# One list scheduler for a whole fused kernel: attention, experts and MLP ordered in three parts with shared state

## The chip, the cores and the metric

The kernel runs on one core of a Trainium2 chip. The metric is the device time of one execution in microseconds, median of several runs on the same chip. Before the change it is 509.02 us (three runs, 508.78 to 509.10). The engines are named as in the profile: PE (matrix products), PEld (loading of the stationary operand), DVE (vector), ACT (activations), POOL, and SP, whose queue starts the transfers.

## What is computed

Three layers follow each other, all in float32, for 4 batches of 448 tokens with 768 features (12 heads of 64):

```python
# attention, capped scores
scores = cap * tanh(q @ k.T * scale / cap)
attn = exp(scores - max) / (sum + 1e-9)
x = (attn @ v) with the heads side by side          # 4 x 448 x 768
# four experts, the best two of each token, causal attention of width 64 inside each expert
w = softmax over the two largest of x @ w_gate
ye = softmax(causal(scale * (x wq[e]) @ (x wk[e]).T)) @ (x wv[e]) @ wo[e]
out = sum over the two experts of w * ye
# gated MLP
h = gelu(out @ w_in); u, v = halves of h
v_n = layernorm(v) * g_ln;  v_s = w_sg @ v_n + b_sg
y = out + (u * v_s) @ w_out
```

## The kernel before

**Attention.** The 48 heads go as 24 pairs, one per `slot`. For a pair, `scores` writes four tiles `s` (three blocks of 128 keys, and one tile with the 64 tail keys of two pairs), ACT turns them into `p` with tanh (one per tile) and exp (one per two tiles), and `values` multiplies `p` with `v` into `po` one slot later. `pb` is the sum of `p` over key blocks (DVE, later POOL), and `sum` is its column sum on PE. Two buffers of PSUM hold `s`, one bank `po`, three the tiles named `g` (`sum`, `w2ps`, `qk`, `v`, `a`, `tr`, `av`, half of the `po`).

**Sub-arrays.** These products use a part of PE's 128 x 128 array and run beside each other: `s` on 64 rows by 128 columns (shown as 64\*128), tail scores and tail values on 64\*64, `po` on 128\*64, `sum` on 128\*32, `a` on 64\*112, `av` on 112\*64. The other products (`w2ps`, `qk`, `v`, and all of the MLP) take the whole array. A float32 product makes two records of the trace ("x4" is two products); `qk`, `v` and the MLP are sums of three products of rounded halves, one record each. A name like `s1_2_3` is batch 1, pair 2, tile 3; `tr0_0_1_2` is batch, expert pair, expert, chunk.

**Beside attention.** In the first 10 slots (`PRE_SLOTS`) `prepare_weights` converts the 64-bit `w_in` in twelve pieces (`wi0` to `wi11`, mostly on DVE) and PE multiplies each with `wo` into `w2ps`. In the slots after that `beside` runs the experts of the batch that is done (`queries_keys` `qk`, `values_chunk` `v`, `gates`, `weigh` `a`, `settle`, `turn` `tr`, `attend` `av`) after the table `PLAN`. `normed` inverts a batch's sums `rs` by way of DRAM (`rd`, `ri`, `rb`) and makes the experts' input `xh`, `xl`.

**What sets the order.** Each engine keeps the order in which the program issues its instructions (`InOrder`, which passes every instruction through one helper line, L338). Up to the last slot that is the order in which the Python code is written. Only the end (`experts_end` and `mlp`, from L1026 on) is recorded in the `Agenda` first: `order` holds estimated durations, buffers (`slots`), the shape that PE is in (`cfg`, 95 ns added where it differs, L226) and PE's bank, walks through estimated time and takes for each engine the instruction that can begin first; within 100 ns of each other PE takes one of the same bank, then the one with the longest chain behind it (`level`, L243). Transfers before the end are outside of it, and its start state is a guess (`since`, L345). All queues are in order: an instruction that waits holds back everything behind it on its engine.

Of the kernel before, what the change touches and what calls it, by code (L numbers as in the profile page):

```python
# [77 lines left out]
class Agenda:  # L78
# [24 lines left out]
    def add(self, eng, f, args, kw):  # L103
# [9 lines left out]
        for x, wr in [(x, False) for x in ins] + [(x, True) for x in outs]:  # L113
            t = x.tensor
            lo, hi, p0, p1 = self.span(x)
            for j, l, h, q0, q1, w in self.seen.setdefault(t.name, []):
                if (wr or w) and lo < h and l < hi and p0 < q1 and q0 < p1 and j != i:
                    after.add(j)
            if t.name not in self.uses:
                self.uses[t.name] = []  # L120
                if x.space != bass.MemoryType.DRAM and getattr(t, "tag", None) is not None:
                    self.caps.setdefault(t.cap_key, []).append((t.name, wr, t))
# [7 lines left out]
        op = dict(i=i, eng=eng, call=lambda: f(*args, **kw), after=after, tiles=set(tiles), took=[], port=False)  # L130
# [3 lines left out]
        if eng == "pe":  # L134
            st, mv = (args[1], args[1]) if name == "transpose" else (kw.get("lhsT", args[1]), kw.get("rhs", args[-1]))
            n = mv.free_size() if name != "transpose" else args[1].partition_size()
            op["dur"] = (96.0 if name == "transpose" else .446 * n + 3.5 if st.dtype == F32R else 2 * max(.825 * n, 185.0))
# [8 lines left out]
        elif eng == "dve":  # L146
# [5 lines left out]
            elif name in ("tensor_scalar", "tensor_copy") and not psum:  # L152
# [5 lines left out]
        else:  # L158
            op["dur"] = 450.0
            size = outs[0].partition_size() * outs[0].free_size() * 4 if outs[0].space != bass.MemoryType.DRAM else (  # L160
                ins[0].partition_size() * ins[0].free_size() * 4)
            op["bytes"] = size
            op["extra"] = 1500.0 if outs[0].tensor.name.startswith(("rb", "ri", "rd", "wo", "gln")) else 0.0
        self.ops.append(op)

    def order(self):
        ops, n = self.ops, len(self.ops)
        then = [[] for _ in ops]
        for op in ops:
            for j in op["after"]:  # L170
                then[j].append(op["i"])
        level = [0.0] * n
        for i in reversed(range(n)):
            op = ops[i]
            took = op["dur"] + self.LATENCY[op["eng"]]
            if op["eng"] == "sp":
# [3 lines left out]
            level[i] = took + max((level[j] for j in then[i]), default=0.0)  # L180
        slots, queue, where, left = {}, {}, {}, {t: len(set(u)) for t, u in self.uses.items()}
        for key, tiles in self.caps.items():
            cap = tiles[0][2].tag_meta.bufs
            old = [t for t, w, _ in tiles if not w]
            slots[key] = [0.0] * (cap - len(old)) + [None] * len(old)
            queue[key] = [t for t, w, _ in tiles if w]
            for t, w, _ in tiles:
                where[t] = (key, len(slots[key]) - 1 - old.index(t) if not w else None)
        need, ready, end = [len(op["after"]) for op in ops], [0.0] * n, [0.0] * n
        for op in ops:  # L190
            for t in op["tiles"]:
                for k, v in self.since.items():
                    if t.startswith(k) and where.get(t, (0, 0))[1] is not None:
                        ready[op["i"]] = max(ready[op["i"]], v)
        open_ = {}
        for t, u in self.uses.items():
            made = {i for i in u if ops[i]["eng"] == "pe" and ops[i]["bank"] == t}
            open_[t] = {j for i in made for j in ops[i]["after"] if ops[j]["eng"] != "pe"} or ({-1} if not made else set())
        feeds = [[] for _ in ops]
        for t, js in open_.items():  # L200
            for j in js - {-1}:
                feeds[j].append(t)
        free = dict.fromkeys(self.LATENCY, 0.0)
        pools = {e: [] for e in free}
        for op in ops:
            if not need[op["i"]]:
                pools[op["eng"]].append(op["i"])
        grid, cfg, bank, lock, pipe, done = [[0.0] * 4 for _ in range(4)], None, None, 0.0, 0.0, []

        def begin(i):  # L210
            op = ops[i]
            t = max(free[op["eng"]], ready[i])
            for x in op["tiles"]:
                key, s = where.get(x, (None, 0))
                if s is not None:
                    continue
                if queue[key][0] != x and (not x.startswith(self.fill) or open_[x] or sum(s is not None for s in slots[key]) < 2):
                    return None
                got = [s for s in slots[key] if s is not None]
# [1062 lines left out]
```

## Time and profile before

| | |
|---|---|
| runs | 508.78, 509.02, 509.10 us |
| profiled execution | 510.37 us, of which the span of the trace is 508.6 us |
| PE | 496.8 us busy (98%) |
| DVE, ACT | 330.8 and 329.0 us (65% each) |
| POOL | 94.2 us (19%) |
| chain that ended last | PE 72%, DVE 12%, ACT 7%, DMA 4% |
| granted PE clock | 1.0 in all slices |

The span is what the trace covers; 1.77 us of the execution lie outside of it. Products on PE overlap and their ends are modelled, so "busy" also hides short stops: the distance from one start to the next tells more than the durations do. Where PE was found idle, the profile names what ended the wait.

### The profile page before, as it was taken

To read this page: it belongs to the slowest core of one execution; us is meant where nothing else is said; L and a number is where in the kernel's file an instruction comes from. 1 tells how busy PE (TensorE), PEld (TensorE's weight loads), DVE (VectorE), ACT (ScalarE), POOL (GpSimd) and SP (SyncE) were. 2 spreads that over 40 slices of the span, in tenths; PEclk is the share of its full clock that TensorE was granted. 3 is DMA by queue.
4 is the path that set the end of the run, shared out by engine and by line. 5 is a ranking of instruction groups with operands and counts; after the bars stand their busy time and mean duration, and the time that the engine had idled before them with its cause. 6 is when DMAs were issued, how large, how long until landed. Compare 5 with 4: busy or idle time off the path is not lost.

```text
span 508.6 us, 7515 instructions
## 1 busy us (share of the span) xinstructions
PE 496.8 (98%) x2702; PEld 329.6 (65%) x2702; DVE 330.8 (65%) x719; ACT 329.0 (65%) x558; POOL 94.2 (19%) x103
## 2 busy tenths in 40 slices
PE   7999999999999999999999989999999999999997
PEld 2233333455555556655559777877799899989996
DVE  4899998992666664655664999847860594497050
ACT  6989989868788686678765757757831263355131
POOL 0000000133145152235063302031410010010000
PEclk9999999999999999999999999999999999999999
DMA  8974626885334142414023622015011001100212
GB/s 292 310 267 141 216 88 141 241 295 176 102 102 151 58 129 63 127 58 113 1 68 88 193 60 64 1 46 233 1 37 54 19 1 56 54 0 1 90 43 85
DMA packets 35188, 54.27 MB, mean 107 GB/s; under 512 B 5584, under 2 KB 30160, under 8 KB 35152
## 3 DMA queue, kind: packets, MB, share of 16 engines
q1 hardware_dynamic: 35008, 53.57, 33.4%
q8 instruction: 21, 0.34, 0.3%
q10 hardware_dynamic: 144, 0.23, 0.2%
q14 instruction: 15, 0.12, 0.1%
HBM read 42.04 MB, written 11.75 MB: 106 GB/s over the span
## 4 chain that ended last, share of the span: by engine, by line
PE 72%; DVE 12%; ACT 7%; DMA 4%; SPq 2%; issue 2%; POOL 0%; DVEq 0%; ACTq 0%; POOLq 0%
PE o L338 17%; PE s L338 8%; PE qk L338 8%; PE po L338 8%; PE sp L338 7%; PE v L338 6%; ACT p L338 4%; PE hu L338 3%; DVE pb L338 3%; PE a L338 3%; PE av L338 3%; PE tr L338 2%; DMA rb<-rd 2%; PE hv L338 2%; ACT pe L338 2%
## 5 line engine op out<-in xcount | busy, mean ns | idle before, releaser
L338 ACT ACTIVATE p<-s,tsc 128x896 f32<-128x896 f32 x84 | 80.9, 1006 | 20.3 <-PE s L338 20.0
L338 PE MATMUL s<-qp,kp 64*128 64x448 f32 (+1 forms) x384 | 79.1, 573 | 3.0 <-ACT p L338 3.0
L338 ACT ACTIVATE p<-p,capt 128x1792 f32<-128x1792 f32 (+1 forms) x48 | 77.0, 1603 | 1.1
L338 DVE TENSOR_TENSOR pb<-pb,p 128x896 f32<-128x896 f32 (+1 forms) x48 | 53.2, 1109 | 20.0 <-ACT p L338 10.7
L338 POOL TENSOR_TENSOR pb<-p 128x896 f32<-128x896 f32 x14 | 29.9, 2134 | 166.5 <-PE po L338 94.7
L338 PE MATMUL po<-p,vv 128*64 128x448 f32 x288 | 59.4, 548 | 0.0
L338 PEld LDWEIGHTS s<-qp,kp 64*128 64x128 f32 (+1 forms) x384 | 27.7, 176 | 48.4 <-issue 23.5
L338 ACT ACTIVATE ob<-o 128x448 f32<-128x448 f32 x24 | 12.9, 544 | 53.1 <-PE o L338 49.0
L338 DVE SCALAR_TENSOR_TENSOR vs<-sp,gln,bsg 128x448 f32<-128x448 f32 x16 | 10.6, 680 | 54.9 <-PE sp L338 54.7
L338 PEld LDWEIGHTS po<-p,vv 128*64 128x64 f32 x288 | 18.5, 136 | 37.9 <-issue 34.1
L338 DVE CUSTOM_DVE_ANT_0 a<-a,neg 112x112 f32<-112x112 f32 (+3 forms) x64 | 27.7, 468 | 20.8 <-PE a L338 20.2
L338 ACT ACTIVATE pe<-a,m 112x112 f32<-112x112 f32 (+3 forms) x64 | 31.1, 493 | 11.5 <-DVE m L338 11.5
L338 PE MATMUL qk<-xh,wqk_h 128*128 128x448 f32 x96 | 37.6, 391 | 0.1
L338 PE MATMUL o<-gh,wu_l 128*128 128x448 f32 x96 | 35.0, 365 | 0.0
L338 PE MATMUL o<-gl,wu_h 128*128 128x448 f32 x96 | 35.0, 364 | 0.0
L338 PE MATMUL qk<-xh,wqk_l 128*128 128x448 f32 x96 | 35.0, 364 | 0.0
L338 PE MATMUL o<-gh,wu_h 128*128 128x448 f32 x96 | 34.9, 364 | 0.0
L338 POOL TENSOR_TENSOR rstd<-rstd,mhalf 128x1 f32<-128x1 f32 (+1 forms) x16 | 10.8, 678 | 121.1 <-DVE rstd L338 119.2
L338 POOL TENSOR_SCALAR pe<-pe,cs 112x224 f32<-112x224 f32 (+3 forms) x40 | 24.1, 621 | 45.7 <-DVE cs L338 44.6
L338 PE MATMUL v<-wvg_h,xh 128*112 128x260 f32 x96 | 28.2, 294 | 1.4 <-ACT pe L338 1.3
L338 PE MATMUL v<-wvg_h,xl 128*112 128x260 f32 x96 | 27.1, 283 | 0.0
L338 PE MATMUL v<-wvg_l,xh 128*112 128x260 f32 x96 | 27.1, 282 | 0.0
(237 smaller groups left out, 1083.8 us busy)
## 6 DMA issues: line engine op xcount, KB each, us to landing
rb<-rd SPq DMA_DIRECT2D x24, 224.0 KB, 5.4
out_dram<-ob SPq DMA_DIRECT2D x24, 224.0 KB, 1.9
kp<-in_kT_dram SPq DMA_DIRECT2D x23, 224.0 KB, 3.0
qp<-in_qT_dram SPq DMA_DIRECT2D x23, 224.0 KB, 3.3
vv<-in_v_dram SPq DMA_DIRECT2D x24, 192.0 KB, 3.3
wuw<-in_w_out_dram SPq DMA_DIRECT2D x5, 384.0 KB, 5.0
wud<-wuw SPq DMA_DIRECT2D x10, 192.0 KB, 1.9
ws<-in_wqk_dram SPq DMA_DIRECT2D x4, 384.0 KB, 7.9
```

Source lines behind the costliest of these rows:

```text
L338: return tc.keep_in_program_order(f(*args, **kw))
```

## The change

All instructions are now recorded in the `Agenda`, in three runs that share its state (estimated free times, buffers, the shape and bank of PE, the transfer pipe): the first 10 slots, the slots after them, and the end. In the first two the key that breaks ties is the program's order, in the third it is `level` as before. Transfers are recorded too (SP still takes them in program order within 20 ns). A product that follows another one on PE counts from that one's estimated start and no longer from its end (`past`). Neighbouring products on a part of the array that fit beside each other form a `gang`; its first member may begin only when the inputs of all members are there. A program-order rule for writers of one tile on PE is added, and `settle` splits its work over three engines only in the end, as before. The helper line is L387 after the change.

```diff
             lo, hi, p0, p1 = self.span(x)
             for j, l, h, q0, q1, w in self.seen.setdefault(t.name, []):
-                if (wr or w) and lo < h and l < hi and p0 < q1 and q0 < p1 and j != i:
+                if j != i and (wr or w) and (lo < h and l < hi and p0 < q1 and q0 < p1 or
+                                             wr and w and name == "matmul" and self.ops[j]["eng"] == eng):
                     after.add(j)
...
+    def order(self, new, by_level, floor):
...
                 took = op["dur"] + (0.0 if any(ops[j]["eng"] == "pe" for j in then[i]) else 220.0)
-            level[i] = took + max((level[j] for j in then[i]), default=0.0)
-        slots, queue, where, left = {}, {}, {}, {t: len(set(u)) for t, u in self.uses.items()}
+            op["level"] = took + max((ops[j]["level"] for j in then[i]), default=0.0)
+            op["key"] = op["level"] if by_level else -op["rank"]
...
+        gang, team = {}, []
+        for i in new:
+            op = ops[i]
+            if op["eng"] != "pe":
+                continue
+            r, c, r0, c0 = op["cell"]
+            if (r, c) == (4, 4) or not team or (r, c) != ops[team[0]]["cell"][:2] or any(
+                    abs(r0 - ops[j]["cell"][2]) < r and abs(c0 - ops[j]["cell"][3]) < c for j in team):
+                team = []
+            team.append(i)
+            gang[i] = team
 
         def begin(i):
             op = ops[i]
-            t = max(free[op["eng"]], ready[i])
-            for x in op["tiles"]:
+            t, mates, new_tiles = free[op["eng"]], [i], {}
+            if i in gang and gang[i][0] == i:
+                mates = gang[i]
+                if any("end" not in ops[q] for j in mates for q in ops[j]["after"] if q not in mates):
+                    return None
+                t = max([t] + [self.past(q, j) for j in mates for q in ops[j]["after"] if q not in mates])
+            t = max(t, ready[i])
+            for x in (x for j in mates for x in ops[j]["tiles"]):
...
+            for j in mates if op["eng"] == "pe" else ():
+                r, c, r0, c0 = ops[j]["cell"]
+                if (r, c) != self.cfg and self.cfg:
+                    t = max(t, max(map(max, grid)) + 95.0)
                 else:
                     t = max(t, max(grid[y][x] for y in range(r0, r0 + r) for x in range(c0, c0 + c)))
             if op["port"]:
...
                 if e == "pe":
-                    t, i = max(near, key=lambda x: (ops[x[1]]["bank"] == bank, level[x[1]], -x[1]))
+                    t, i = max(near, key=lambda x: (ops[x[1]]["bank"] == self.bank, ops[x[1]]["key"], -x[1]))
                 elif e == "sp":
                     t, i = min(near, key=lambda x: x[1])
                 else:
-                    t, i = max(near, key=lambda x: (level[x[1]], -x[1]))
-                if best is None or t < best[0]:
+                    t, i = max(near, key=lambda x: (ops[x[1]]["key"], -x[1]))
+                if best is None or t < best[0] + (1.0 if e == "pool" else 0.0):
                     best = (t, i)
...
+    def past(self, j, i):
+        x, a, b = self.ops[j], self.ops[j]["eng"], self.ops[i]["eng"]
+        if a == b == "pe":
+            return x["at"]
+        return x["end"] + (0.0 if a == b and "bytes" not in x else self.LATENCY[a])
+
+    def run(self, by_level, floor=lambda key: 0.0):
...
             for i in range(NC):
                 pe = PES[b, ep, el, i]
-                by = "apavaaap"[4 * el + i] if agenda.on else "p"
+                by = "apavaaap"[4 * el + i] if agenda.end else "p"
                 if by == "a":
                     act.activation(pe, pe, AF.Copy, scale=cs[:, i:i + 1])
                 elif by == "v":
@@ -1011,8 +1060,12 @@
             for _ in range(int(WARM)):
                 mm(g, z[:, :128], z, start=True, stop=True)
         load_w, beside_pre = prepare_weights(pre)
+        agenda.on = True
+        agenda.free["pe"] = 3400.0
         for n in range(PRE_SLOTS):
             slot(n, beside_pre(n))
+        agenda.run(False, )
+        used = max(op["end"] for op in agenda.ops)
     ypool = ES(tc.tile_pool(name="ypool", bufs=3, reuse_waits="tile"))
     mo = ES(tc.tile_pool(name="mo", bufs=1, reuse_waits="tile"))
     sm = ES(tc.tile_pool(name="sm", bufs=2, reuse_waits="tile"))
@@ -1020,10 +1073,14 @@
     w2_t = [w2.tile([128, 2, FF], F32R, name=f"w2_{t}") for t in "hl"]
     w2_h, w2_l = w2_t
     YA = {}
+    agenda.on = True
     for n in range(PRE_SLOTS, B * HP + 1):
         slot(n, beside(n))
+    agenda.run(False, lambda key: used if str(key).split("_")[-2] in ("mo", "ypool", "w2") else 0.0)
+    closed = max(op["end"] for op in agenda.ops if any(t.startswith(("p", "kp", "s")) for t in op["tiles"]))
     ah.close()
-    agenda.on = True
+    agenda.on = agenda.end = True
+    agenda.fill = tuple(f"{t}{b}" for t in "ov" for b in range(B))
 
 
 
@@ -1222,7 +1279,7 @@
     agenda.hold(("wo", "wu_"), ("wqk", "wvg"))
     drain(mlp(((mlp_a, 0), (token_weights, 0), (mlp_weights, 2), (mlp_b, 0), (mlp_weights, 1), (mlp_a, 1), (mlp_b, 1),
                (mlp_a, 2), (mlp_b, 2), (mlp_a, 3), (mlp_b, 3), (mlp_c, 0), (mlp_c, 1), (mlp_c, 2), (mlp_c, 3))))
-    agenda.run()
+    agenda.run(True, lambda key: closed if str(key).split("_")[-2] in ("ml", "w4", "mr", "ps") else 0.0)
 
 
 def _rows(w):

```

Three places on PE show what the planner does. The first is the start of the program, from the tail scores of the first two pairs (`s0_0_3`) on; before:

```order
L338 MATMUL s0_0_3_172<-qp0_1_125,kp0_1_126 64x448 x2
L338 MATMUL s0_1_0_186<-qp0_1_125,kp0_1_126 128x448 x2
L338 MATMUL s0_1_1_190<-qp0_1_125,kp0_1_126 128x448 x2
L338 MATMUL po0_0_208<-p0_0_0_135,vv0_0_121 64x448 x4
L338 MATMUL po0_0_208<-p0_0_1_167,vv0_0_121 64x448 x2
L338 MATMUL s0_1_2_220<-qp0_1_125,kp0_1_126 128x448 x2
L338 MATMUL s0_2_0_232<-qp2_131,kp2_132 128x448 x2
L338 MATMUL s0_2_1_236<-qp2_131,kp2_132 128x448 x2
L338 MATMUL po0_0_208<-p0_0_1_167,vt0_0_123 64x448 x2
```

After:

```order
L387 MATMUL s0_0_3_130<-qp0_1_114,kp0_1_115 64x448 x2
L387 MATMUL po0_0_140<-p0_0_0_119,vv0_0_112 64x448 x4
L387 MATMUL s0_1_0_134<-qp0_1_114,kp0_1_115 128x448 x2
L387 MATMUL s0_1_1_135<-qp0_1_114,kp0_1_115 128x448 x2
L387 MATMUL po0_0_140<-p0_0_1_128,vv0_0_112 64x448 x2
L387 MATMUL po0_0_140<-p0_0_1_128,vt0_0_113 64x448 x2
L387 MATMUL po0_1_155<-p0_0_1_128,vt0_0_113 64x448 x2
L387 MATMUL s0_1_2_144<-qp0_1_114,kp0_1_115 128x448 x2
L387 MATMUL s0_2_0_148<-qp2_117,kp2_118 128x448 x2
```

The first values (`po0_0`, `po0_1` with the tail operand `vt`) moved ahead of the scores of pair 1 and of `s0_1_2`, in two pieces.

The second is about slot 8, where the products `w2ps` of the last pieces of `w_in` stand. Before, from the last score tile of pair 2 of batch 1:

```order
L338 MATMUL s1_2_3_691<-qp8_497,kp8_498 64x448 x2
L338 MATMUL s1_2_3_691<-qp9_564,kp9_565 64x448 x2
L338 MATMUL w2ps1_0_552<-wi9m_577,wt_108 128x512
L338 MATMUL w2ps1_1_553<-wi9m_577,wt_108 128x512
L338 MATMUL sum1_0_700<-pb1_0_520,onehot_71 32x448 x2
L338 MATMUL sum1_0_700<-pb1_1_590,onehot_71 32x448 x2
L338 MATMUL s1_3_0_715<-qp9_564,kp9_565 128x448 x2
L338 MATMUL s1_3_1_719<-qp9_564,kp9_565 128x448 x2
L338 MATMUL po1_2_734<-p1_2_0_640,vv1_2_605 64x448 x4
L338 MATMUL po1_2_734<-p1_2_1_686,vv1_2_605 64x448 x2
L338 MATMUL s1_3_2_752<-qp9_564,kp9_565 128x448 x2
L338 MATMUL w2ps1_0_552<-wi10m_609,wt_108 128x512
```

After, from the tile ahead of it:

```order
L387 MATMUL s1_2_3_271<-qp8_219,kp8_220 64x448 x2
L387 MATMUL s1_2_3_271<-qp9_237,kp9_238 64x448 x2
L387 MATMUL w2ps1_0_234<-wi10m_251,wt_108 128x512
L387 MATMUL w2ps1_0_234<-wi11m_260,wt_108 128x512
L387 MATMUL w2ps1_1_235<-wi11m_260,wt_108 128x512
L387 MATMUL po1_0_248<-p1_0_1_231,vt1_0_210 64x448 x2
L387 MATMUL po1_1_266<-p1_0_1_231,vt1_0_210 64x448 x2
L387 MATMUL po1_1_266<-p1_1_0_239,vv1_1_230 64x448 x4
L387 MATMUL po1_1_266<-p1_1_1_253,vv1_1_230 64x448 x2
L387 MATMUL sum1_0_272<-pb1_0_226,onehot_71 32x448 x2
L387 MATMUL sum1_0_272<-pb1_1_246,onehot_71 32x448 x2
L387 MATMUL s1_3_0_277<-qp9_237,kp9_238 128x448 x2
```

The products of `wi10` and `wi11` moved from behind `s1_3_2` to directly behind `s1_2_3`, and the values `po1_0`, `po1_1` from ahead of `s1_2_2` to behind them. On DVE the conversion of `wi11` now stands among the adds for `pb1_1`, with the subtraction `wqk_l` ahead of its end.

The third is in the experts of batch 0, second expert pair, where `qk0_1_0` and the transposes of the first pair `tr0_0_0` meet. Before:

```order
L338 MATMUL tr0_0_0_2_1282<-ident_73,pe0_0_0_2_1087 112x112 x3
L338 MATMUL qk0_1_0_1268<-xh0_745,wqk_h_76 128x448
L338 MATMUL qk0_1_0_1268<-xh0_745,wqk_l_77 128x448
L338 MATMUL qk0_1_0_1268<-xh0_745,wqk_h_76 128x448
L338 MATMUL qk0_1_0_1268<-xh0_745,wqk_l_77 128x448
L338 MATMUL tr0_0_0_3_1291<-ident_73,pe0_0_0_3_1121 112x112 x4
L338 MATMUL qk0_1_0_1268<-xh0_745,wqk_h_76 128x448
L338 MATMUL qk0_1_0_1268<-xh0_745,wqk_l_77 128x448
L338 MATMUL qk0_1_0_1268<-xl0_746,wqk_h_76 128x448 x6
L338 MATMUL sum2_0_1306<-pb2_0_972,onehot_71 32x448 x2
L338 MATMUL sum2_0_1306<-pb2_1_1097,onehot_71 32x448 x2
L338 MATMUL s2_3_0_1332<-qp15_1068,kp15_1069 128x448 x2
```

After:

```order
L387 MATMUL qk0_1_0_906<-xh0_285,wqk_l_77 128x448
L387 MATMUL qk0_1_0_906<-xl0_286,wqk_h_76 128x448 x6
L387 MATMUL tr0_0_0_0_908<-ident_73,pe0_0_0_0_835 112x112
L387 MATMUL tr0_0_0_0_908<-ident_73,pe0_0_0_1_846 112x112 x2
L387 MATMUL tr0_0_0_2_909<-ident_73,pe0_0_0_2_864 112x112 x3
L387 MATMUL s2_3_0_916<-qp15_856,kp15_857 128x448 x2
L387 MATMUL tr0_0_0_3_910<-ident_73,pe0_0_0_3_876 112x112 x4
L387 MATMUL sum2_0_911<-pb2_0_838,onehot_71 32x448 x2
L387 MATMUL sum2_0_911<-pb2_1_869,onehot_71 32x448 x2
L387 MATMUL s2_3_1_917<-qp15_856,kp15_857 128x448 x2
```

The transposes, which stood in three places among the products of `qk0_1_0`, now stand behind all 18 of them, and a score tile (`s2_3_0`) stands between two transposes and ahead of `sum2_0`.

## Rows read from the trace of the kernel before

**Rows 1.** The page, busy time of each engine over the whole span.
```profile
PE 496.8 (98%) x2702; PEld 329.6 (65%) x2702; DVE 330.8 (65%) x719; ACT 329.0 (65%) x558; POOL 94.2 (19%) x103
```

**Rows 2.** Busy time by stretch: its width, then each engine's busy us and instructions.
```profile
60.00:80.00 20.00, 20.00 (x97) 6.72 (x94) 19.25 (x31) 17.72 (x21) 0.00 (x0) 1.00 0.29 86
180.00:200.00 20.00, 19.55 (x130) 12.61 (x132) 9.39 (x26) 14.77 (x26) 10.44 (x13) 1.00 0.35 105
200.00:220.00 20.00, 19.67 (x129) 10.45 (x126) 10.36 (x34) 14.66 (x24) 7.59 (x10) 1.00 0.37 104
```

**Rows 3.** Timeline of PE at startup: start, duration (us), run of instructions, idle before it.
```profile
8.43 1.28 PE L338 MATMUL s<-qp,kp 64*64 64x448 f32 x8 [0.32 <-ACT p L338]
...
11.15 1.92 PE L338 MATMUL s<-qp,kp 64*128 64x448 f32 x8 [1.44 <-ACT p L338]
...
18.38 1.02 PE L338 MATMUL s<-qp,kp 64*128 64x448 f32 x4 [1.20 <-ACT p L338]
```

**Rows 4.** Timeline of PE, runs of products, each ahead of one of another shape.
```profile
49.81 1.02 PE L338 MATMUL s<-qp,kp 64*128 64x448 f32 x4
50.77 1.98 PE L338 MATMUL w2ps<-wi4m,wt 128*128 128x512 f32 x4
...
54.40 1.77 PE L338 MATMUL s<-qp,kp 64*128 64x448 f32 x8
56.10 0.98 PE L338 MATMUL po<-p,vt 64*64 64x448 f32 x8
57.01 2.48 PE L338 MATMUL po<-p,vv 128*64 128x448 f32 x12
59.42 1.94 PE L338 MATMUL s<-qp,kp 64*128 64x448 f32 x12
```

**Rows 5.** Timeline of PE and its weight loads, the first sums behind the experts' start.
```profile
102.28 1.98 PE L338 MATMUL sum<-pb,onehot 128*32 128x448 f32 x8
...
103.30 0.14 PEld L338 LDWEIGHTS sum<-pb,onehot 128*32 128x32 f32 x4 [0.89 <-DVE pb L338]
...
104.18 1.77 PE L338 MATMUL s<-qp,kp 64*128 64x448 f32 x8
```

**Rows 6.** Timeline of PE, transposes between products of `qk`.
```profile
144.18 0.45 PE L338 MATMUL tr<-ident,pe 112*112 112x112 f32 x3
144.41 0.45 PE L338 MATMUL qk<-xh,wqk_h 128*128 128x448 f32 x1
144.69 0.36 PE L338 MATMUL qk<-xh,wqk_l 128*128 128x448 f32 x1
144.89 0.36 PE L338 MATMUL qk<-xh,wqk_h 128*128 128x448 f32 x1
```

**Rows 7.** Timeline of PE in the last part, three of its waits.
```profile
295.36 0.36 PE L338 MATMUL hu<-yh,w_l 128*128 128x448 f32 x1
296.11 0.98 PE L338 MATMUL a<-qk 64*112 64x224 f32 x8 [0.39 <-ACT pt L338]
...
298.60 0.45 PE L338 MATMUL tr<-ident,pe 112*112 112x112 f32 x3
300.39 0.37 PE L338 MATMUL v<-wvg_h,xh 128*112 128x260 f32 x1 [1.33 <-ACT pe L338]
...
359.48 0.97 PE L338 MATMUL tr<-ident,pe 112*112 112x112 f32 x8
360.99 0.38 PE L338 MATMUL tr<-ident,pe 112*112 112x112 f32 x2 [0.54 <-ACT pt L338]
```

**Rows 8.** Timeline of PE and DVE, products of `w_in` and its last conversion.
```profile
79.67 1.98 PE L338 MATMUL w2ps<-wi9m,wt 128*128 128x512 f32 x4
...
80.95 0.69 DVE L338 TENSOR_TENSOR wi11m<-wi11m,wi11e 128x512 f32<-128x512 f32 x1
...
82.56 0.95 DVE L338 TENSOR_TENSOR wqk_l<-ws,wqk_h 128x768 fp32r<-128x768 f32 x1
...
89.36 1.88 PE L338 MATMUL w2ps<-wi11m,wt 128*128 128x512 f32 x4
```

More of the change, by code (lines that the diff above doesn't have):

```diff
@@ L82, with __init__ @@
     OVERLAP = {"act": 100.0, "dve": 80.0, "pool": 27.0, "sp": 0.0}
-    def __init__(self, tc, since):
-        self.tc, self.since = tc, since
-        self.ops, self.on = [], False
+    def __init__(self, tc):
+        self.tc = tc
+        self.ops, self.on, self.late, self.end = [], False, 0, False
         self.seen, self.uses, self.caps = {}, {}, {}
-        self.behind, self.fill = {}, tuple(f"{t}{b}" for t in "ov" for b in range(B))
+        self.behind, self.fill = {}, ()
+        self.slots, self.queue, self.where, self.left = {}, {}, {}, {}
+        self.free = dict.fromkeys(self.LATENCY, 0.0)
+        self.grid = [[0.0] * 4 for _ in range(4)]
+        self.cfg = self.bank = None
+        self.lock = self.pipe = 0.0
+        self.last, self.kept = {}, set()
     def hold(self, these, those):
@@ new lines, in order @@
+        slots, queue, where, left = self.slots, self.queue, self.where, self.left
+        keep = {t for tiles in self.caps.values() for t, _, _ in tiles[-tiles[0][2].tag_meta.bufs:]}
+        for t, u in uses.items():
+            left[t] = len({i for i in u if "end" not in ops[i]}) + (t in keep)
+            if t in self.kept and not left[t] and where.get(t, (0, None))[1] is not None:
+                key, s = where[t]
+                slots[key][s] = max(ops[j]["end"] for j in u)
+        self.kept = keep
@@ L197, in order @@
+        need, ready = {}, {}
+        for i in new:
+            need[i] = sum("end" not in ops[j] for j in ops[i]["after"])
+            ready[i] = max([0.0] + [self.past(j, i) for j in ops[i]["after"] if "end" in ops[j]])
+        open_, feeds = {}, {i: [] for i in new}
+        for t, u in uses.items():
             made = {i for i in u if ops[i]["eng"] == "pe" and ops[i]["bank"] == t}
-            open_[t] = {j for i in made for j in ops[i]["after"] if ops[j]["eng"] != "pe"} or ({-1} if not made else set())
@@ L208, in order @@
-        grid, cfg, bank, lock, pipe, done = [[0.0] * 4 for _ in range(4)], None, None, 0.0, 0.0, []
+        for i in new:
+            if not need[i]:
+                pools[ops[i]["eng"]].append(i)
+        gang, team = {}, []
+        for i in new:
+            op = ops[i]
[7 more added lines that the diff above has]
+            gang[i] = team
@@ L214, in begin @@
+            t = max(t, ready[i])
+            for x in (x for j in mates for x in ops[j]["tiles"]):
                 key, s = where.get(x, (None, 0))
[L215 removed]
+                if s is not None or x not in queue[key]:
                     continue
[L217 to L219 removed]
```

138 lines of the change are left out of this document (68 added, 70 removed).

## Prediction

> **What bounds the kernel now.** I read the busy shares first: PE is busy 98% of the span, DVE and ACT 65% [rows 1]. So the end is set by how much time PE's list of products takes, and by the few waits in it; there are some 12 us of idle PE in 508.6. Then the table by stretches: it shows where another engine is near its limit. From 60 to 80 us DVE is busy 19.25 of 20 us and ACT 17.72, with PE at 20.00; later DVE has half of its time free, and PE still loses 0.45 and 0.33 us in two stretches [rows 2]. Last the timeline of PE, from start to start, since its ends are modelled: it shows which waits there are (three at startup, one at the first sums, three large ones in the last part) [rows 3, 5, 7], and what PE itself pays for the order of its products [rows 4, 6]. A reader should see that the change can win only the waits, and that it can lose by putting shapes in a worse order, because most of the time there is nothing on PE to fill.
>
> **What a change of shape costs.** Two products `s` with their two records each take 0.96 us to the next start, four of them 1.70: the second two took 0.74, so 0.22 of the 0.96 is the change to another shape. The eight records of tail values run four at a time, 0.74 at that pace, and take 0.91: 0.17. The twelve of `po`, two at a time, would take 6 x 0.37 = 2.22 and take 2.41: 0.19 [rows 4]. I take 0.19 us a change, with 0.15 and 0.23 as ends. A transpose run between products of `qk` is no such change, but the next product takes 0.28 to its successor, not 0.20 [rows 6]: 0.08 at most, and 0 at least if the transposes in front, which are only 0.23 apart for three, got it back. I take 0.05, the nearer to what the row shows.
>
> Counted in the order of PE's instructions, shape changes go from 162 to 178: +4 at startup, -2 to slot 10, +15 from there to the end of batch 3's sums, -1 after. So the grouping does not group shapes overall; a score tile or `tr` now stands between others as in the third place shown. Against this, about 18 interruptions by transposes go.
>
> The Trainium skill speaks against this change here: "TensorEngine Tiling (Array Packing)", section Key Properties, says that changing the tiling mode, and not just the tile, drains TensorE. By it the 16 added changes cost and a transposition among whole-array products costs nothing, so that nothing would come back for the 18: the sum would be 0.9 us worse, 508.1. The rows agree on the first half and not on the second, since the product behind the transposes shows 0.08 more [rows 6].
>
> **Up to slot 10 (about 104 us).** At startup PE waits 0.32, 1.44 and 1.20 us for ACT's `p`, which frees the score buffers [rows 3]. Now `po0_0` (four products, four steps of 0.37 = 1.48) stands in front of `s0_1_0`, as long as the second wait; its other two and four tail values stand in front of `s0_1_2` and cover the third. Their inputs, the first two `p` and `vv0_0`, are what the waiting scores wait for anyway. I take 1.44 + 1.20 = 2.64 as gone and 0.32 as staying; 0 to 2.96 as ends. Four more changes cost 0.76; net -1.9. The two changes less to slot 10: -0.4. At the first sums of batch 1 behind the experts' start, the eight records take 1.90 from start to start, and the second half waits for DVE's `pb`; undisturbed 0.89 would be near (0.74 and a change): 1.0 lost [rows 5]. The chain in front (inverted sums, `os`, `xh`) begins earlier on DVE and SP now; -0.8, ends 0 and -1.0.
>
> New is a wait for the conversion of `w_in`. Before, `w2ps` of `wi11` started at 89.36, and its operand was ready at 81.64 (80.95 + 0.69) [rows 8]: 7.7 us of slack. Now it stands behind `s1_2_3`, whose place is 79.67 before. Ahead of it have come four products more (1.98 + 1.88, as their rows have it, less the overlap: about 3.7) and gone the values `po1_0` tail and `po1_1` (0.91 + 2.41 = 3.3 [rows 4]); with the 2.3 us won before, PE is there at 79.67 + 3.7 - 3.3 - 2.3 = 77.8. DVE has a subtraction of 0.95 more ahead of the end [rows 8]: 82.6, if it gains nothing itself. But DVE too waited for `p` of the scores that now come 1.9 earlier, and it leaves 0.75 of 20 us idle in the stretch shown [rows 2], some 2.3 in three of them by estimate: if both are saved, it ends at 82.6 - 1.9 - 2.3 = 78.4. The wait is 0.6 to 4.8, or 0 if the scheduler has left other adds behind; behind it on PE stand `po1_0`, `po1_1`, the sums and the scores of pair 3, so ACT's tanh would run dry. I take 1.5, nearer to the low end, as DVE's adds follow the earlier scores. Sum of the part: -1.9 - 0.4 - 0.8 + 1.5 = -1.6.
>
> **From slot 10 to the end of attention.** 15 changes x 0.19 = +2.9; 18 interruptions x 0.05 = -0.9. PE is full there, so both count in full, whatever DVE and ACT do. The idle 0.45 + 0.33 [rows 2], waits for `v` and `tr` buffers, should be filled by score tiles that are drawn forward: -0.8, ends 0 and -0.8. The transposes of the first pair wait for `settle`, and on DVE a piece of w_out's conversion now precedes the factors: a wait up to 1.56 as for the worst chain seen [rows 7], but 16 products of `qk` (16 x 0.20 = 3.2) have come in front too; +0.4. Sum: +1.6.
>
> **The end.** The three waits are 296.11 - 295.36 - 0.20 = 0.55, of which about 0.2 is the change of shape; 300.39 - 298.60 - 0.23 = 1.56, for exponentials of `a2_1` whose chain takes 300.39 - 296.11 = 4.28; and 360.99 - 359.48 - 8 x 0.08 = 0.87 [rows 7]. The 72 products of `v3`, which stood behind the second, are now ahead of `hu0_0`, so behind `a2_1` there is what there was (three transposes, six products of `hu0_1`, three transposes) and four transposes (0.32): the wait becomes about 1.2. The other two have no such chain in the new order that I find; I take 0.35 + 0.87 as gone, ends 0 and all. One change less: -0.2. Sum: -0.36 - 1.22 - 0.2 = -1.8.
>
> **The sum.** -1.6 + 1.6 - 1.8 = -1.8 us. The profiled execution took 510.37, 1.35 more than the median of the runs, so it would go to 508.6; the runs, which I forecast, from 509.02 to 507.2. The DVE, ACT and POOL lists hold the same work in another order; it stays beside PE save where a wait is named above. What is next when waits go is PE itself.
>
> **Rivals.**
> *All waits seen go and none comes.* -1.9 - 0.3 - 0.4 - 1.0, then +1.2, then -2.8 - 0.2: -5.4, 503.6; with changes at 0.15 and 0.08 for each interruption a further 1.2, 502.4. For it: the scheduler knows the shape, the buffers and the bank. Against: its durations are guesses, and DVE's limit before 82 us is real.
> *The change gives back what it wins* (it does not group, as the count of shapes says). The first part goes as above, -1.6, but the waits of the middle (so 2.9 - 0.9 + 0.4 = +2.4) and the two others of the end (-0.36 - 0.2 = -0.6) stay where their chains are: +0.2, 509.2, no change. For it: in neither place do I see in the new order what would fill them.
> *DVE sets the first part*, slower. Place: the two products of `wi11`. If DVE ends that piece at 82.6, PE waits 4.8, all that was won before is lost, and the sums behind, on the same DVE queue, wait as before: -2.3 + 4.8 + 1.6 - 1.8 = +2.3, 511.3. It decides from a wait of 3.5 us (-2.3 + 3.5 - 0.2 = +1.0). For it: DVE at 96% there. Against: DVE's waits for `p` shrink with PE's lead.
>
> **Chances.** Forecast (505.5 to 508.8) 0.42, all waits go 0.16, given back 0.21, DVE first 0.21. About 0.2%, 1.0 us, is what a measurement can tell here: faster is below 508.0, slower above 510.0. Faster: 0.16 and most of 0.42, in all 0.54; within: the rest of it and most of the second rival, 0.23; slower: the third and a little, 0.23. The range for 8 in 10 is 502.5 to 511.2, its own for the likeliest case 505.5 to 508.8.
>
> **What would show it.** Right: the scores behind `po0_0` start without the 1.44 and 1.20; `w2ps` of `wi11` shows an idle time before it, released by DVE, of 1 to 2 us at 77 to 80; the first sums take about 0.9; the windows from 100 to 270 hold PE at 20.00 with fewer products done per stretch; the wait behind `a2_1` is 1.2. Wrong: a PE idle sum above 12 us, a wait over 3.5 at `wi11`, score tiles late by ACT in 20 to 60 us, or a stretch from 104 to 270 that becomes shorter in spite of 15 more shapes, which would mean that a change costs less than 0.15.

## The result: slower, by 1.1%

The changed kernel takes 514.9 us (512.39 to 516.54, four runs) against 508.9 of the kernel before; the ratio is 1.011 (1.0077 to 1.0143). Measured again in five rounds it took 514.1 us, ratio 1.0093 (1.0073 to 1.0113). The forecast was 507.2, range 502.5 to 511.2. The rows below named "after" are those of its fastest execution, 512.39 us with a span of 510.6; the other three had spans of 512.7 to 514.8 and a mean granted clock of 0.993 to 0.997.

PE's share did not move, its busy time rose from 496.8 [rows 1] to 500.4 us:

```profile
PE 500.4 (98%) x2702; PEld 328.7 (64%) x2702; DVE 328.2 (64%) x719; ACT 327.8 (64%) x558; POOL 90.7 (18%) x103
```

The starts on PE in both traces show where the 2.0 us of span came from: of each run of like products, its length to the next start, less the pace of its products; of what is left, the usual amount for such a change of product is counted as the price of the order, the rest as waiting. Only the sum of the two is read directly; the split is an estimate, as it hangs on what is taken as usual. The table sums this for the traces at a granted clock of 1.0 in all slices (us). Much of its waiting is short stops for which PE's rows name no releaser: the idle times that they name, without the warm-up, add up to 6.6 us before and 5.1 after.

| | before | after |
|---|---|---|
| price of the order on PE (162 and 178 shape changes, and transposes in between) | 28.7 | 30.8 |
| waits up to the third tile of pair 1 and behind it (startup) | 5.3 | 2.3 |
| waits at the first `qk` (96 to 104 us) | 1.3 | 2.2 |
| waits from there to batch 3's sums | 1.5 | 1.2 |
| waits in the end, the tail included | 5.8 | 8.0 |
| all waits | 13.9 | 13.8 |

So by this count the order costs 2.1 us more, and the waits won at the start were lost at the first `qk` and in the end. What the other executions have on top is a second thing, found in the first experiments.

The startup, timeline of PE (start, duration, run, idle before it and its releaser), answers to [rows 3]: 0.35 and 0.19 us idle in place of 0.32, 1.44 and 1.20.

```profile
6.95 2.77 PE L387 MATMUL s<-qp,kp 64*128 64x448 f32 x12 [0.35 <-ACT p L387]
...
11.32 1.77 PE L387 MATMUL s<-qp,kp 64*128 64x448 f32 x8
13.28 0.97 PE L387 MATMUL po<-p,vv 128*64 128x448 f32 x4 [0.19 <-ACT p L387]
```

The first `qk` and the sums behind it, timeline of PE, answers to [rows 5]. The sums now take 0.89 from start to start instead of 1.90, as foreseen; but the products of `qk` in front of them wait twice, 0.81 and 1.05 us, for the last third of `xh` and `xl`.

```profile
96.41 0.98 PE L387 MATMUL s<-qp,kp 64*64 64x448 f32 x8
98.21 0.47 PE L387 MATMUL qk<-xh,wqk_h 128*128 128x448 f32 x1 [0.81 <-DVE xh L387]
...
101.15 0.68 PE L387 MATMUL qk<-xl,wqk_h 128*128 128x448 f32 x2 [1.05 <-DVE xl L387]
101.75 0.96 PE L387 MATMUL sum<-pb,onehot 128*32 128x448 f32 x8
102.64 1.77 PE L387 MATMUL s<-qp,kp 64*128 64x448 f32 x8
```

DVE in that time: an add for `pb` stands between the last multiplication `os` and the cast; the cast takes 0.63, and the subtraction for `xl` behind it 2.90 us, where such a subtraction takes 1.09:

```profile
95.29 1.08 DVE L387 TENSOR_TENSOR os<-os,rb 128x896 f32<-128x896 f32 x1
96.41 1.09 DVE L387 TENSOR_TENSOR pb<-pb,p 64x896 f32<-64x896 f32 x1
97.53 0.63 DVE L387 CAST xh<-os 128x896 fp32r<-128x896 f32 x1
98.19 2.90 DVE L387 TENSOR_TENSOR xl<-os,xh 128x896 fp32r<-128x896 f32 x1
```

POOL in that time, the add that began the sum of pair 4 of batch 1:

```profile
97.63 2.51 POOL L387 TENSOR_TENSOR pb<-p 128x896 f32<-128x896 f32 x1 [95.97 <-ACT p L387]
```

The two waits of 0.45 and 0.33 us for `v` and `tr` [rows 2] are gone (behind the width of the stretch, PE's busy us):

```profile
180.00:200.00 20.00, 20.00 (x132) 12.40 (x131) 12.35 (x33) 14.75 (x27) 9.89 (x13) 1.00 0.25 80
200.00:220.00 20.00, 20.00 (x129) 10.98 (x128) 11.44 (x34) 14.52 (x23) 7.81 (x10) 1.00 0.37 107
```

### The profile page after: what moved, and what is told of

It is laid out like the page before. It is cut to its first block, busy times and chain, and to the rows that moved or that the text cites. A ratio compares the mean times of both kernels' runs of the same rounds, so it can differ in the third digit from the quotient of the medians.

```text
span 510.6 us, 7536 instructions
## 1 busy us (share of the span) xinstructions
PE 500.4 (98%) x2702; PEld 328.7 (64%) x2702; DVE 328.2 (64%) x719; ACT 327.8 (64%) x558; POOL 90.7 (18%) x103
## 4 chain that ended last, share of the span: by engine, by line
PE 85%; DVE 8%; ACT 4%; DMA 1%; issue 1%; SPq 0%; POOL 0%; ACTq 0%; DVEq 0%; POOLq 0%
PE o L387 16%; PE s L387 13%; PE po L387 12%; PE qk L387 11%; PE v L387 7%; PE sp L387 6%; PE w2ps L387 4%; PE a L387 3%; PE av L387 3%; PE hv L387 3%; PE tr L387 3%; PE hu L387 2%; PE sum L387 2%; ACT pe L387 1%; ACT p L387 1%; DMA rb<-rd 1%
## 5 line engine op out<-in xcount | busy, mean ns | idle before, releaser
L387 ACT ACTIVATE p<-s,tsc 128x896 f32<-128x896 f32 x84 | 82.8, 1010 | 26.3 <-PE s L387 24.9
L387 PE MATMUL s<-qp,kp 64*128 64x448 f32 (+1 forms) x384 | 81.2, 575 | 0.3 <-ACT p L387 0.3
L387 ACT ACTIVATE p<-p,capt 128x1792 f32<-128x1792 f32 (+1 forms) x48 | 77.3, 1611 | 1.1
L387 DVE TENSOR_TENSOR pb<-pb,p 128x896 f32<-128x896 f32 (+1 forms) x48 | 53.2, 1108 | 26.0 <-ACT p L387 25.4
L387 PE MATMUL po<-p,vv 128*64 128x448 f32 x288 | 59.9, 548 | 0.2 <-ACT p L387 0.2
L387 POOL TENSOR_TENSOR pb<-p 128x896 f32<-128x896 f32 x14 | 30.2, 2159 | 164.2 <-ACT p L387 164.1
L387 DVE CUSTOM_DVE_ANT_0 a<-a,neg 112x112 f32<-112x112 f32 (+3 forms) x64 | 27.9, 470 | 45.0 <-PE a L387 42.8
L387 PEld LDWEIGHTS s<-qp,kp 64*128 64x128 f32 (+1 forms) x384 | 26.6, 174 | 44.9 <-issue 26.5
L387 ACT ACTIVATE ob<-o 128x448 f32<-128x448 f32 x24 | 12.8, 544 | 52.7 <-PE o L387 47.9
L387 PEld LDWEIGHTS po<-p,vv 128*64 128x64 f32 x288 | 18.4, 136 | 38.5 <-issue 33.9
L387 DVE SCALAR_TENSOR_TENSOR vs<-sp,gln,bsg 128x448 f32<-128x448 f32 x16 | 10.7, 680 | 48.9 <-PE sp L387 48.9
L387 ACT ACTIVATE pe<-a,m 112x112 f32<-112x112 f32 (+3 forms) x64 | 31.0, 490 | 11.5 <-DVE m L387 7.9
L387 PE MATMUL qk<-xh,wqk_h 128*128 128x448 f32 x96 | 36.6, 382 | 0.9 <-DVE xh L387 0.8
L387 PE MATMUL o<-gl,wu_h 128*128 128x448 f32 x96 | 35.1, 366 | 0.0
L387 PE MATMUL o<-gh,wu_l 128*128 128x448 f32 x96 | 35.1, 365 | 0.0
L387 PE MATMUL qk<-xh,wqk_l 128*128 128x448 f32 x96 | 34.9, 364 | 0.0
L387 PE MATMUL o<-gh,wu_h 128*128 128x448 f32 x96 | 34.8, 364 | 0.0
L387 POOL TENSOR_TENSOR rstd<-rstd,mhalf 128x1 f32<-128x1 f32 (+1 forms) x16 | 11.4, 712 | 115.0 <-DVE rstd L387 115.0
L387 POOL TENSOR_SCALAR pe<-pe,cs 112x224 f32<-112x224 f32 (+3 forms) x40 | 22.9, 593 | 47.3 <-DVE cs L387 46.9
L387 PE MATMUL v<-wvg_h,xh 128*112 128x260 f32 x96 | 27.8, 289 | 0.1
L387 PE MATMUL v<-wvg_h,xl 128*112 128x260 f32 x96 | 27.1, 283 | 0.0
L387 PE MATMUL v<-wvg_l,xh 128*112 128x260 f32 x96 | 27.1, 282 | 0.0
```

What stands on the lines that cost most here:

```text
L387: return tc.keep_in_program_order(f(*args, **kw))
```

## Experiments

"Order of the kernel before" means that the recorded instructions of a part are issued in that order, by an explicit list, while the planner's estimates run on as before (cuts are marked by `...`):

```diff
+        new = [op["i"] for op in self.ops if "end" not in op]
+        order = self.order(new, by_level, floor)
+        kept = order if by is None else by(new)
...
+        for i in kept:
...
-        agenda.run(False, )
+        agenda.run(False, by=lambda new: new)
...
-    agenda.run(True, lambda key: closed if str(key).split("_")[-2] in ("ml", "w4", "mr", "ps") else 0.0)
+    agenda.run(True, lambda key: closed if str(key).split("_")[-2] in ("ml", "w4", "mr", "ps") else 0.0,
+               by=lambda new: [new[k] for k in END])
```

With all three lists, PE, DVE, ACT and POOL would have the order of the kernel before, and SP program order; that kernel was not run.

| kernel | what is new in it | median us | ratio to before (interval) |
|---|---|---|---|
| again | all | 514.10 | 1.0093 (1.0073 to 1.0113) |
| only_p1 | first 10 slots | 510.94 | 1.0032 (1.0019 to 1.0044) |
| only_p2 | slots 10 to 24 | 515.49 | 1.0122 (1.0108 to 1.0137) |
| not_p3 | all but the end | 512.92 | 1.0071 (1.0058 to 1.0084) |
| same_dve | all, one add on DVE | 511.56 | 1.0054 (1.0042 to 1.0066) |
| before_dve | nothing but that add | 511.51 | 1.0055 (1.0035 to 1.0075) |
| p1_dve | first 10 slots, that add | 507.68 | 0.9974 (0.9965 to 0.9983) |
| shape_dve | all, that add, shape first | 523.40 | 1.0277 (1.0249 to 1.0305) |
| p12_dve | all but the end, that add | 510.44 | 1.0033 (1.0021 to 1.0045) |
| tail_dve | same_dve, tail in program order | 510.81 | 1.0036 (1.0022 to 1.0050) |

**Which part costs what.** Four kernels. Expected of the first, the changed kernel once more:

> The changed kernel once more. By the ledger of its first trace (shape changes +2.1 us; waits -3.1 at the start, +1.0 at the first qk, -1.1 at 190 to 205, +3.1 in the end and the tail) the order alone gives about +2 to +3.5 us over the kernel before at a granted clock of 1.0, and each execution with a granted clock below 1.0 is longer by (1 - clock) x span, so 0.995 is +2.6. Rival: the scatter is not the clock's, and executions at a clock of 1.0 scatter as widely, 512 to 516.

Of the start alone (second run with `by=lambda new: new`, end by `END`):

> The first 10 slots in the new order, the other two parts in the instruction order of the kernel before (SP in program order throughout). Ledger: three waits at startup go and four shape changes come, -2.8 us: 506 us. Rival (DVE sets the first part): the lead is lost before the first qk at 98, within 0.5 us of before. Rival (the order on SP costs): slower than before by 1 us or more, as then all kernels with the new SP order are.

Of the middle alone (first run `by=lambda new: new`, end by `END`):

> Only slots 10 to 24 in the new order, start and end in the instruction order of the kernel before. Ledger: 15 more shape changes less 18 interruptions, +2, and the wait at qk0_0_0 for xh and xl, +1 to +1.7, less the two waits for v and tr, -1.1: +2 to +3, 511 to 512 us. Rival (shape changes are hidden anyway): within 0.5 us of before.

Of all but the end:

> The first two parts in the new order, the end in the instruction order of the kernel before. Ledger: the end and its tail cost the change +1.6 us, so this is 1.6 faster than the changed kernel at the same clock, about 509.5. If the lower granted clock comes from the new start or middle, some executions show it here too; if from the new end, none do. Rival: the end is not worse by itself but by where it starts, then this is as slow as the changed kernel.

Of `again`, the two executions at a granted clock of 1.0 took 512.07 and 513.23, 3.0 and 4.2 over the kernel before, and the four below it 514.03 to 515.18; of the 2 to 3.5 expected at 1.0 one is inside and one above. The clock is below 1.0 in all executions of `only_p2` and `not_p3` and in eight of twelve of `only_p1` (510.70 to 511.79, against 508.69 to 509.89 at 1.0), so the lower clock is not the new end's.

The end costs 1.2 us (514.10 to 512.92), near what was expected: the intervals of the two ratios overlap, but at a clock below 1.0 the executions do not, 514.03 to 515.18 against 511.94 to 513.37. The start alone is slower than before instead of 2.8 faster, and the middle alone costs twice the 2 to 3 expected. The three parts alone cost 1.9, 6.4 and 1.2, together 9.5, where the whole costs 5.1: the start alone and the middle alone each pay the wait that follows.

In all four traces the same place differs from the first trace. In `again`, PE:

```profile
96.28 0.98 PE L387 MATMUL s<-qp,kp 64*64 64x448 f32 x8
100.11 0.47 PE L387 MATMUL qk<-xh,wqk_h 128*128 128x448 f32 x1 [2.84 <-DVE xh L387]
...
101.07 0.58 PE L387 MATMUL qk<-xh,wqk_l 128*128 128x448 f32 x1
101.44 2.44 PE L387 MATMUL qk<-xl,wqk_h 128*128 128x448 f32 x6
```

PE waits 2.84 us for `xh`, and the products behind run at a slower pace, 0.37 from start to start instead of 0.20. The stretches around them show the granted clock, the third column from the end (PE's busy us behind the width of the stretch):

```profile
98.00:100.00 2.00, 0.00 (x0) 0.00 (x0) 2.00 (x1) 1.97 (x3) 1.57 (x1) 1.00 0.90 280
100.00:101.00 1.00, 0.89 (x3) 0.83 (x4) 0.97 (x2) 1.00 (x1) 0.00 (x0) 0.76 0.57 202
101.00:102.00 1.00, 1.00 (x4) 0.88 (x4) 0.18 (x1) 0.22 (x1) 0.00 (x0) 0.50 0.67 194
...
103.00:104.00 1.00, 1.00 (x7) 0.46 (x9) 0.00 (x0) 0.08 (x1) 0.00 (x0) 0.53 1.03 364
104.00:105.00 1.00, 1.00 (x10) 0.27 (x4) 0.09 (x1) 0.47 (x1) 0.00 (x0) 1.00 0.95 365
```

The clock falls to 0.50, the lower of the two levels (1.2 GHz instead of 2.4), within about a microsecond of PE taking up work again (in `only_p2` just ahead of it: PE starts at 102.53, and 102 to 103 has a mean of 0.63), and is back at 1.00 some 3 us later. The same is seen in `only_p1` behind 2.22 us of idle time, in `not_p3` behind 3.25 and in `only_p2` behind 2.77; in the first trace, with 0.81 and 1.05, and in the kernel before, it stays at 1.00. So one wait is paid twice: as idle time, and as some 1.5 us of slower products (the ten up to the sums take 3.70 us in `again`, 2.22 in the kernel before). In `only_p1`:

```profile
100.52 0.47 PE L484 MATMUL qk<-xh,wqk_h 128*128 128x448 f32 x1 [2.22 <-DVE xh L484]
```

DVE and POOL in `again` show what PE waits for; the cast of 0.62 takes 2.40 us, while POOL's add runs from 97.49 to 99.57:

```profile
96.54 1.09 DVE L387 TENSOR_TENSOR pb<-pb,p 64x896 f32<-64x896 f32 x1
97.66 2.40 DVE L387 CAST xh<-os 128x896 fp32r<-128x896 f32 x1
100.09 1.09 DVE L387 TENSOR_TENSOR xl<-os,xh 128x896 fp32r<-128x896 f32 x1
```

```profile
97.49 2.08 POOL L387 TENSOR_TENSOR pb<-p 128x896 f32<-128x896 f32 x1 [95.84 <-ACT p L387]
```

In `only_p1` it is DVE's add in front of the cast that takes 2.89 beside POOL's. On this the Trainium skill, page "Perfetto Trace Analysis", section Optimizing Scalar/DVE Operations, says that GPSIMD and DVE share an SBUF read port. The trace agrees here, 2.40 against 0.62 us. The same stands in the trace before, a multiplication of 2.44 us beside POOL's add, and the prediction left it out.

**Is it POOL's add?** Each engine in the order of the changed kernel, one instruction moved:

```diff
-            (dve if b == 0 or (b, hp) < (1, 4) else pool_e).tensor_tensor(pb, p[:, :, 0, :], p[:, :, 1, :], op=ALU.add)
+            (dve if b == 0 or (b, hp) < (1, 5) else pool_e).tensor_tensor(pb, p[:, :, 0, :], p[:, :, 1, :], op=ALU.add)
```

> The changed kernel, every engine in the order of the changed kernel, but the first add for pb1_4 (1.08 us on DVE, 2.08 on POOL) is DVE's, behind its last xl, and not POOL's. Theory (POOL's add holds DVE's last cast to xh or subtraction to xl, which take 2.4 to 2.9 us in place of 0.62 and 1.09; PE waits for them 2.8 us, and its clock halves behind the wait): the cast takes 0.62 again, PE's wait for it is about 1 us, the granted clock stays 1.0, and the time falls by 3 to 3.5 us, to about 511. Rival (the transfer of rb is late, the add is innocent): wait and clock stay, 514.

511.56, 2.5 us faster than `again`; PE's wait is 0.98, and the granted clock 1.0 over the whole span. The add for `pb` in front of the cast is still there, 1.09 us, about what PE still waits; no run moved that one. PE, then DVE:

```profile
98.14 0.47 PE L561 MATMUL qk<-xh,wqk_h 128*128 128x448 f32 x1 [0.98 <-DVE xh L561]
```

```profile
97.45 0.63 DVE L561 CAST xh<-os 128x896 fp32r<-128x896 f32 x1
98.12 1.09 DVE L561 TENSOR_TENSOR xl<-os,xh 128x896 fp32r<-128x896 f32 x1
```

The control, the kernel before with that add on DVE:

> The kernel before with the same add on DVE, as a control. There POOL's add stretches the multiplication by rb2 from 1.09 to 2.44 us, but PE has score tiles to do in that time and waits only 0.4 and 1.0 us. Theory: some 0.5 us faster, 508.5; rival (DVE's extra 1.08 us is what counts there): slower by up to 1 us.

It was 2.4 us slower, against both expectations, and not for either's reason: in this build SP issues a load of `wqk` (`ws`) two places later, behind `kp` and `qp`, since transfers are outside of the kept order there. ACT waits 3.81 us for it, and PE 2.20 behind ACT:

```profile
115.92 0.84 ACT L338 ACTIVATE wqk_h<-ws 128x768 fp32r<-128x768 f32 x1 [3.81 <-DMA ws<-in_wqk_dram]
```

```profile
118.94 0.78 PE L338 MATMUL a<-qk 64*112 64x224 f32 x3 [2.20 <-ACT pe L338]
```

Behind these 2.20 us the granted clock, third from the end, stays at 1.00:

```profile
119.00:122.00 3.00, 2.75 (x17) 1.25 (x18) 0.81 (x4) 3.00 (x7) 1.02 (x1) 1.00 0.65 213
```

The waits at the first `qk` and sums themselves fell from 1.4 to about 0.4. As a control of the add alone it is spoiled.

With the start alone:

> Only the first 10 slots in the new order, the rest in the instruction order of the kernel before, and the add for pb1_4 on DVE. Theory: the start's gain of 2.8 us is no longer lost at the first qk (4.0 us of waits there in only_p1, 1.3 in the kernel before), so 510.9 - 2.7 - about 0.5 of clock: 506.5 to 507.5, faster than the kernel before. Rival (the lead is lost to DVE or to transfers anyway): 509 to 511 as in only_p1.

507.68, 3.3 us less than `only_p1` and faster than the kernel before. PE's wait at the first `qk` is 1.18, the clock 1.0:

```profile
99.15 0.47 PE L484 MATMUL qk<-xh,wqk_h 128*128 128x448 f32 x1 [1.18 <-DVE xh L484]
```

This is the only version that beats both kernels, by 0.26% (0.17 to 0.35) against the kernel before. With the control spoiled, how much of it is the start's and how much the add's is not separated. All but the end, with the add on DVE (`same_dve` with the end by `END`):

> The first two parts in the new order with the add for pb1_4 on DVE, the end in the instruction order of the kernel before. By the ledger of the traces: same_dve less what the new end costs (shape changes -0.6, waits +2.2, together 1.6 to 1.9), so 509.7 to 510; and against p1_dve (507.7) the new middle costs its shape changes, +1.9 by starts, less the waits at 190 to 205, -1.1, plus what differs at the first qk, about +1: 509.5 to 510. Rival (the end is slow only because of where it starts): as slow as same_dve, 511.5.

510.44: the end costs 1.1, less than expected, and the middle 2.8 against `p1_dve`, more. Its ten runs fall into two groups, 509.9 to 510.6 and 511.1 to 512.3; of the four slower ones two have a clock of 0.996, so the clock alone does not make the group. The traced one, 512.3, had a wait of 2.31 us there without any work on POOL, since DVE waited 0.78 us for `rb2` and the add for `pb` came in front of the cast, and its clock halved too:

```profile
99.79 0.69 PE L561 MATMUL qk<-xh,wqk_h 128*128 128x448 f32 x1 [2.31 <-DVE xh L561]
```

In this trace a late transfer was enough. In `p1_dve` DVE waited 0.74 us for the same transfer, but PE came to the first `qk` at 96.09 instead of 94.68, and waited 1.18.

**Are fewer shape changes worth it?**

```diff
-                    t, i = max(near, key=lambda x: (ops[x[1]]["bank"] == self.bank, ops[x[1]]["key"], -x[1]))
+                    t, i = max(near, key=lambda x: (ops[x[1]]["cell"][:2] == self.cfg, ops[x[1]]["bank"] == self.bank,
+                                                    ops[x[1]]["key"], -x[1]))
```

> The changed kernel with the add on DVE, and among PE's instructions that can begin within 100 ns the planner takes one of PE's present shape first, then as before one of the same bank. Shape changes fall from 178 to 155 by count. Theory (0.19 us each, nothing hides them): 23 x 0.19 = 4.4 us less than same_dve, if the waits stay, about 506.5. Rival (what is saved in changes comes back as waits, since other work is put off): as slow as same_dve.

It was the slowest of all, 523.4. By the count of starts its order costs 2.9 us less than that of the changed kernel (27.9 against 30.8), but the waits go from 12.7 in `same_dve` to 28.8 us, since products that feed ACT and DVE are put off. The lower clock is in these 28.8: a mean granted clock of 0.987 over a span of 522.7 us is, by estimate, 6.8 us. (The planner ordered all engines anew here, with the add on DVE, so that not only PE's order differs from `same_dve`.) The largest wait is 2.80 us for `xh` at the first `qk`, with nothing on POOL; the next is one for exponentials, and behind it PE runs at the lower clock for all of 352 to 358 us. It does so for some 3 us behind a third one too, of only 1.23:

```profile
312.87 1.09 PE L387 MATMUL tr<-ident,pe 112*112 112x112 f32 x7 [1.23 <-ACT pe L387]
...
351.38 1.49 PE L387 MATMUL tr<-ident,pe 112*112 112x112 f32 x7 [2.71 <-ACT pe L387]
```

```profile
314.00:317.00 3.00, 3.00 (x10) 0.94 (x12) 2.71 (x13) 1.99 (x6) 0.00 (x0) 0.55 0.14 46
...
352.00:358.00 6.00, 6.00 (x22) 2.83 (x24) 3.23 (x12) 3.56 (x9) 1.31 (x3) 0.50 0.00 0
```

**The tail.** The last 69 instructions in program order:

```diff
+    END = END[:1779] + sorted(END[1779:])
```

> same_dve with its last 69 instructions in program order: the five products of o3_2 that stood behind the 18 of o3_4 go back in front of o3_3. Theory: they kept a PSUM bank and put two evictions and two output transfers in a row at the very end, 0.7 us of wait on PE and more behind the last product; 511.56 - 1.1 = 510.4. Rival: the end is set by the transfers, no difference.

510.81, 0.75 us faster (by starts, 1.0 of PE's tail goes). By the times alone this is not clear: the intervals of the two ratios overlap, and four of its eight executions, 511.2 to 512.1, are like the five of `same_dve`, 511.4 to 511.9. In the changed kernel the eviction of `o3_2` starts at 502.62 with that of `o3_3`, a third waits for an output transfer, and PE for a bank:

```profile
502.62 0.98 ACT L387 ACTIVATE ob<-o 128x448 f32<-128x448 f32 x2 [7.88 <-PE o L387]
...
503.21 0.47 PE L387 MATMUL o<-yh,wo_h 128*128 128x448 f32 x1 [0.68 <-ACT ob L387]
...
505.21 0.55 ACT L387 ACTIVATE ob<-o 128x448 f32<-128x448 f32 x1 [1.62 <-DMA out_dram<-ob]
```

In `tail_dve` they come one product group apart:

```profile
501.21 0.55 ACT L561 ACTIVATE ob<-o 128x448 f32<-128x448 f32 x1 [3.15 <-PE o L561]
...
504.86 0.54 ACT L561 ACTIVATE ob<-o 128x448 f32<-128x448 f32 x1 [3.10 <-PE o L561]
```

## Why the prediction was wrong

Two steps failed. Between the traces of the kernel before and of `again` the time grew by 3.7 us where -1.8 was forecast. By starts, the first `qk` with its clock makes some 3.8 of these 5.5 us and the end some 3.3; the wait for `wi11` that did not come takes 1.5 off.

**The step that failed first** is the one on the first sums: "The chain in front (inverted sums, `os`, `xh`) begins earlier on DVE and SP now; -0.8". It was +0.9 in the first trace and +3.1 in `again`, the slower clock behind it included. The chain did begin earlier, its last `os` at 95.29 and 95.42 instead of 96.90:

```profile
96.90 2.44 DVE L338 TENSOR_TENSOR os<-os,rb 128x896 f32<-128x896 f32 x1 [0.85 <-DMA rb<-rd]
```

But it ended no earlier. An add for `pb` of 1.09 us now stands in front of the cast, and POOL's add stretches the cast or the subtraction by 1.8 us, where it stretched `os` by 1.35 before. In the first trace `xl` was ready at 101.09 (101.12 before), in `again` `xh` at 100.06 (100.00 before), while PE arrives some 2 us earlier. So the sentence that the lists of DVE, ACT and POOL hold "the same work in another order; it stays beside PE save where a wait is named above" failed too: it put their new order at nothing. In the kernel before PE started that third's products at 100.06, ahead of the sums of [rows 5]:

```profile
100.06 0.47 PE L338 MATMUL qk<-xh,wqk_h 128*128 128x448 f32 x1
```

After the change it did so at 98.21 in the fastest execution and at 100.11 in `again`. What PE had won at the start it lost waiting there. I priced the wait as time only; that the clock falls behind a wait of 2 to 3 us was in no row of the kernel before, whose waits are at most 1.44 [rows 3, 7].

**The mechanism of the slower rival was right, its place wrong.** DVE does set the first part, but at `xh`, not at `wi11`. There the products start 77.74 as worked out (77.8), without a wait, for DVE was done at 75.5 and not at 78.4 to 82.6. PE, then DVE:

```profile
77.74 1.88 PE L387 MATMUL w2ps<-wi11m,wt 128*128 128x512 f32 x4
```

```profile
74.80 0.69 DVE L387 TENSOR_TENSOR wi11m<-wi11m,wi11e 128x512 f32<-128x512 f32 x1
```

That was not because other adds went behind it: 107 instructions stand ahead of it on DVE in both kernels, the same but for one. In the kernel before, the steps of a piece follow each other, each in need of the one before it, and start 0.03 us behind its end (median of 61 pairs). The new order mixes the steps of two pieces, and such a step starts 0.08 us before the end of its neighbour (median of 42); by estimate that is 42 x 0.11 = 4.6 us. DVE, before and after:

```profile
79.03 0.69 DVE L338 SCALAR_TENSOR_TENSOR wi11m<-wi_5w,wi11m 128x512 int32<-128x512 int32 x1
79.76 0.43 DVE L338 TENSOR_SCALAR wi11e<-wi11m 128x512 int32<-128x512 int32 x1
```

```profile
66.02 0.68 DVE L387 SCALAR_TENSOR_TENSOR wi10m<-wi_4w,wi10m 128x512 int32<-128x512 int32 x1
66.62 0.42 DVE L387 TENSOR_SCALAR wi11m<-wi11m 128x512 int32<-128x512 int32 x1
```

Up to there the time in which DVE is at work falls from 68.9 to 64.6 us, and its idle time from 12.6 to 10.9. The prediction had only the second.

**The end** was forecast at -1.8 and came out at +1.6 (shapes -0.6, waits +2.2). The three waits of [rows 7] went or fell, but new ones came, and the prediction priced only the places where the kernel before waited. In two of three places the eight `a` take 1.44 us to the next start where they took 0.91 and 0.76. PE's row names no wait there, but the loading of their operand (PEld) stops for 0.41 us, until DVE has the maximum `m` of an earlier one. And a wait of 0.80 is new:

```profile
304.60 1.51 PE L387 MATMUL a<-qk 64*112 64x112 f32 x8
305.48 0.27 PEld L387 LDWEIGHTS a<-qk 64*112 64x112 f32 x2 [0.41 <-DVE m L387]
...
306.04 0.50 PE L387 MATMUL tr<-ident,pe 112*112 112x112 f32 x3
...
347.30 0.50 PE L387 MATMUL tr<-ident,pe 112*112 112x112 f32 x3 [0.80 <-ACT pe L387]
```

Of the 2.2, 1.1 is the tail, which the prediction did not price. In the times of the runs the end costs less than in the traces, 1.1 to 1.2, but does not win 1.8.

**What held.** The start: -1.9 foreseen, -2.2 by starts, of which -3.0 in waits and +0.8 in order. The price of the order: +2.2 foreseen in all, +2.1 by the count of starts, of which the split is an estimate. The prediction's other reading, in which only changes of shape cost, would have given +3.1; a count of this kind does not decide between the two. For the change itself the Trainium skill, "TensorEngine Tiling (Array Packing)", section Key Properties, says that changing the tiling mode drains TensorE. The trace agrees, with 0.17 to 0.22 us a change [rows 4]. The waits at 190 to 205 went, and `tr0_0` did not wait. That the medians differ by 5 to 6 us and the first two traces by 2.0 is in part the executions: the traced one of the kernel before was 1.35 above its median, that of the changed kernel its fastest. What made the former slower stays open, and so does what decides whether the clock falls behind a wait.

## What to carry to other kernels

Work that is moved forward on the engine that sets the time wins only if the next operand that it needs moves forward too: look for the first chain of transfers and vector work behind the place, and price the wait there, not only at the waits that the old order had. Do this for every place at which the new order differs, the tail included. A planner that counts products and changes on one engine, and guesses at the rest, can trade cheap changes of shape (0.19 us) for dear waits: in `shape_dve` 2.9 us won by the count of starts, 16 lost, the lower clock included.

## What was not expected of the hardware

Waits of 2.2 to 3.3 us on PE were followed in five traces by some 3 us at a granted clock of 0.50; in `shape_dve` one of 2.80 was too, one of 2.71 by over 6 us, and one of only 1.23 by some 3, while one of 1.49 was not. And behind 2.20 us in `before_dve` and 1.55 in `tail_dve` the clock stayed at 1.00, so the length of the wait alone does not decide it. What does is not shown.

A cast on DVE of 0.62 us took 2.40 beside a POOL add of 2.08, ending 0.5 us behind it, and both engines can be stretched: in `only_p1` POOL's add took 3.87 and DVE's 2.89 us. And a DVE instruction that does not need its neighbour's result started some 0.1 us sooner than one that does: 0.08 us before the neighbour's end instead of 0.03 behind it.
